# Where the second banks of maxima stand in the attention loop, and how VectorE takes them in the odd slot

## The chip, the core and the metric

The kernel runs on one core of a Trainium2 chip. The metric is the device time of one execution in microseconds. Three runs of the kernel before gave 723.34, 723.61 and 723.65 us; their median is 723.61.

## The reference, cut to what matters

One token mixer with a sliding window, gated by a channel MLP. S = 2048 tokens, D = 512 channels, 32 heads of 16 channels, a window of 256 tokens, 1792 hidden channels.

```
xn = layernorm(x)
q, k, v = split(xn @ wqkv)                       # 32 heads of 16
scores = q @ k^T * 16**-0.5, masked to 0 <= i - j < 256
s = softmax(scores) @ v, heads joined, @ wo
g = silu(gelu(layernorm(xn) @ w1 + b1) @ w2 + b2)
out = x + s * g
```

The change touches one part: the largest score of each query row. The softmax subtracts it, so it must be known before the probabilities of that row are made.

## The kernel before

The attention works on groups of four heads (n = 0 to 7) and blocks of 128 tokens (16 in a group). A query block sees three key blocks: its own, the one before and the one two before; the outer two are masked so that together they make one full block. So 128 units "group, block" run through three stages.

**Maxima** (lines 570 to 592). The scores of one block of queries for four heads go into two tiles of PSUM, of two banks each. The tile `xy` holds three of four parts of each bank pair; `max_first` fills it with matmuls, then VectorE copies the masked half of one block over the other (`copy_predicated`, 128x256) and reduces 768 columns to 6 maxima (`tensor_reduce`). The tile `zo` holds the rest; `max_second` fills columns 0 to 255 of both its banks, and VectorE does the same with a copy of 256 columns and a reduce of 256 columns to 2 maxima. `a` is the index of the bank. The last 256 columns of bank 1 of `zo` are `otb`, the place of the output product. The text calls `xy` the first banks and `zo` the second banks.

**Probabilities** (`prob_part`). TensorE makes transposed scores in the tile `stb`, ScalarE takes the exponential into `pt`, GpSimd zeroes what the mask excludes.

**Output product** (`pv_part`). TensorE multiplies `pt` by the values `vt` into `otb`, and ScalarE copies it to `oraw`, which goes to DRAM.

The loop (line 988) makes one pass u for two blocks, with an even slot t = 2u and an odd slot t = 2u + 1; `pv_part(u)` ends the pass. The maxima run `LEAD` = 12 blocks ahead, so passes 0 to 57 each hold two blocks of maxima. Before the loop, `max_block` does the first 12 blocks. Between these steps the loop spreads fills (`fb`), the projections and other matmuls that TensorE does on the side; `parted` cuts their list into pieces, and `some` issues one. Steps put off by `later` are issued by `run(delayed.pop(...))`; `planned` issues copies and fetches by a table of due times.

The order is written out by hand: the wrapper at line 42 issues each instruction and keeps it in the order of the program on its engine. So line 42 stands in nearly all rows of the profile, and the tiles tell the instructions apart. Semaphores come from the tile library, which sees a tile such as `zo` in its waits.

In the even slot, the order on TensorE was: scores, first banks, a piece of the fills, second banks, more fills. On VectorE: copy of xy, copy of zo, reduce of zo, reduce of xy. In the odd slot TensorE does a piece of fills, second banks, fills, first banks, then the next pass's scores and the output product; VectorE does copy of zo, reduce of zo, copy of xy, reduce of xy.

Of the kernel before, what the change touches and what calls it, by code (L numbers as in the profile page):

```python
# [13 lines left out]
ALU = mybir.AluOpType  # L14
AX = mybir.AxisListType
# [3 lines left out]
P = 128  # L19
# [6 lines left out]
LEAD = 12  # L26
# [23 lines left out]
def mixer_kernel(ctx, tc, x, wqk, wv, wo, w1, b1, w2, b2, out):  # L50


    nc = SimpleNamespace(**{name: Ordered(tc, name) for name in ("tensor", "vector", "scalar", "gpsimd", "sync")})
# [94 lines left out]
    def run(steps):  # L148
        for step in steps:
            step()  # L150
# [31 lines left out]
    zo = psum.tile([P, 2, 512], F32, name="zo")  # L182
# [40 lines left out]
    mask = upper.bitcast(I32).unsqueeze(1).to_broadcast([P, 2, P])  # L223
# [61 lines left out]
    now = [0, 0]  # L285
    delayed = {}
# [263 lines left out]
    def max_place(n, qb):  # L550

        if (n, qb // 4) not in mts:
            mts[n, qb // 4] = small.tile([P, 2, 2, 2, 4], F32, tag="mt", name=f"mt_{n}_{qb}", bufs=2)
        return mts[n, qb // 4].rearrange("q a p i b -> q a (p i) b")[:, :, :, qb % 4]

    def max_scores(out, n, qb, p, parts):

        slot = slots[n % 2]
        for at_, first, count, step in parts:
            for a in (1, 0):  # L560
                r = slice(64 * a, 64 * a + 64)
                row = slot[r, 1, p]
                if first is None:
                    keys = row[:, 0:1].to_broadcast([64, P * count])
                else:
                    keys = row.rearrange("d (b k) -> d b k", k=P)[:, first: first + step * (count - 1) + 1: step]
                nc.tensor.matmul(out[:, a, P * at_: P * (at_ + count)], slot[r, 0, p, P * qb: P * (qb + 1)], keys,
                                 start=True, stop=True)

    def max_second(n, qb):  # L570

        max_scores(zo, n, qb, 1, [(0, qb - 2, 2, 2)] if qb > 1 else [(0, 0, 2, 1)] if qb else [(0, None, 1, 1), (1, 0, 1, 1)])
        own = zo[:, :, P: 2 * P]
        nc.vector.copy_predicated(own, mask, zo[:, :, 0: P])
        nc.vector.tensor_reduce(out=max_place(n, qb)[:, :, 3], in_=own, axis=AX.X, op=ALU.max, negate=True)

    def max_first(n, qb):

        max_scores(xy, n, qb, 0, [(0, qb - 2, 3, 1)] if qb > 1 else [(0, 0, 1, 1), (1, 0, 2, 1)] if qb else
                   [(0, None, 2, 1), (2, 0, 1, 1)])  # L580
        max_scores(xy, n, qb, 1, [(3, qb - 1 if qb else None, 1, 1)])
        nc.vector.copy_predicated(xy[:, :, 2 * P: 3 * P], mask, xy[:, :, 0: P])
        return lambda: nc.vector.tensor_reduce(
            out=max_place(n, qb)[:, :, 0:3], in_=xy[:, :, P: 4 * P].rearrange("q a (i k) -> q a i k", k=P),
            axis=AX.X, op=ALU.max, negate=True)

    def max_block(n, qb):

        rest = max_first(n, qb)
        max_second(n, qb)  # L590
        rest()

    def max_rows(n, c, t):
# [25 lines left out]
    def prob_part(u, part):  # L619

        n, kb = u // 8, 2 * (u % 8)
        if part == 2 and kb == 14:
            return
        slot = slots[n % 2]
        both = stb[0]
        if 16 * n + kb + LEAD >= 16 * NQ and (3 * u + (part + 3) % 3) % 2:
            both = xy
        pt = pp.tile([P, 2, 512], F32, tag="pt", name=f"pt_{u}_{part}")

        def scores(at_, a, p, k, q, w):  # L630
            r = slice(64 * a, 64 * a + 64)
            nc.tensor.matmul(both[:, a, at_: at_ + w], slot[r, 1, p, P * k: P * (k + 1)],
                             slot[r, 0, p, P * q: P * q + w], start=True, stop=True)
        if part < 2:
            w = min(384, S - P * kb)
            for a in (1, 0):
                scores(128, a, part, kb, kb, w)
            for a in (1, 0):
                scores(0, a, part, kb + 1, kb + 1, 128)
            w += 128  # L640
        else:
            w = 512
            for p in range(2):
                for a in (1, 0):
                    scores(256 * p, a, p, kb + 1, kb + 2, 256)
        outs["exp"] = nc.scalar.activation(pt[:, :, 0:w], both[:, :, 0:w], AF.Exp, scale=DH ** -0.5)

        def select(at_, step, pattern, compare, by):
            nc.gpsimd.affine_select(out=at_, in_=at_, pattern=pattern, compare_op=compare, fill=0.0, base=0,
                                    channel_multiplier=by)  # L650
        if part < 2:
            own = pt[:, :, 0:256].rearrange("k a (b q) -> k a b q", b=2)
            select(own, 1, [[0, 2], [0, 2], [1, P]], ALU.is_ge, -1)
            if w == 512:
                select(pt[:, :, 384:512], 1, [[0, 2], [-1, P]], ALU.is_gt, 1)
        else:
            last = pt.rearrange("k a (p q) -> k a p q", p=2)[:, :, :, 128:256]
            select(last, 1, [[0, 2], [0, 2], [-1, P]], ALU.is_gt, 1)
        pts[u, part] = pt
# [154 lines left out]
    n, raw = raws["qk"]  # L814
    nc.gpsimd.tensor_tensor(wqs[0][:, 1], raw, wqs[0][:, 0].bitcast(F32), op=ALU.subtract)
    for j, (raw, cast) in enumerate(zip(raws["v"], (nc.scalar.copy, nc.gpsimd.tensor_copy))):
        cast(wva[:, 0, 2 * j: 2 * j + 2], raw)
        nc.gpsimd.tensor_tensor(wva[:, 1, 2 * j: 2 * j + 2], raw, wva[:, 0, 2 * j: 2 * j + 2].bitcast(F32),
                                op=ALU.subtract)
# [114 lines left out]
    def fill_in(t, half):  # L934
        now[:] = t, half
        run(delayed.pop((t, half), ()))
        for fn, args in fills.get((t, half), ()):
            fn(*args)

    def planned(t):  # L940
        for fn, args in plan.get(t, []):
            fn(*args)

    def ended(t):
        for fn, args in ends.get(t, []):
            fn(*args)

    end = 16 * NQ

    def own_max(part, m):  # L950
        return part(m // 16, m % 16) if m < end else lambda: None

    def own_rows(m, t):
        if 0 <= m < end and m % 4 == 3:
            max_rows(m // 16, m % 16 // 4, t)

    for t in range(-16, 0):
        m = t + LEAD
        if t == -5:
            open_slot(1)  # L960
            for k in range(4):
                at(-4 + k // 2 * 2, clear_part, k)
        fill_in(t, 0)
        planned(t)
        if 4 <= m < LEAD:
            max_block(0, m)
        fill_in(t, 1)
        if t == -1:
            early.close()
            stb.append(attn.enter_context(tc.tile_pool(name="ps_s2", bufs=1, space=PSUM)).tile(  # L970
                [P, 2, 512], F32, name="stb"))
            prob_part(0, 0)
            fill_in(t, 2)
        if 0 <= m < 4:
            max_block(0, m)
        run(lns.get(t, ()))
        own_rows(m, t)
        ended(t)
    def parted(todo, *cuts):

        n = sum(fn.__name__ == "unit" for fn, _ in todo)
        at_ = [0, *(-(-n * k // 20) for k in cuts), len(todo)]
        return [todo[a: b] for a, b in zip(at_, at_[1:])]

    def some(todo):
        for fn, args in todo:
            fn(*args)
    for u in range(end // 2):
        t = 2 * u
        prob_part(u, 1)  # L990
        rest = own_max(max_first, t + LEAD)
        calm[0] = t < end - LEAD
        even, odd = (fills.pop((v, 0), []) for v in (t, t + 1))
        if u % 8:
            parts = parted(even, 5) + parted(odd, 10 if u % 8 == 7 else 5, 20)
        else:
            parts = parted(even + odd, 2, 6, 10, 14)
        now[:] = t, 0
        run(delayed.pop((t, 0), ()))
        some(parts[0])  # L1000
        own_max(max_second, t + LEAD)
        rest()
        planned(t)
        some(parts[1])
        fill_in(t, 1)
        ended(t)
        t += 1
        prob_part(u, 2)
        now[:] = t, 0
        run(delayed.pop((t, 0), ()))  # L1010
        some(parts[2])
        own_max(max_second, t + LEAD)
        some(parts[3])
        planned(t)
        fill_in(t, 1)
        own_max(max_first, t + LEAD)()
        calm[0] = False
        own_rows(t + LEAD, t)
        for fn, args in todo_dve:
            fn(*args)  # L1020
        todo_dve.clear()
        if u % 8:
            some(parts[4])
        if t + 1 < end:
            prob_part(u + 1, 0)
        if u % 8 == 0:
            some(parts[4])
        fill_in(t, 2)
        pv_part(u)
        ended(t)  # L1030
# [29 lines left out]
    for f in range(6, NF, 2):  # L1060
        t = gp.tile([P, 2, 512], F32, tag="ohl", name=f"hr_{f}", bufs=4)
# [452 lines left out]
```

## Time and profile before

| | us |
|---|---|
| median of three runs | 723.61 |
| the profiled execution | 723.22 |
| its span, first to last instruction | 721.1 |
| stretch 60 to 385 (most of the attention loop): TensorE busy | 318.98 of 325.00 |
| the same stretch: VectorE busy | 270.00 |
| the same stretch: ScalarE busy | 237.86 |
| the same stretch: GpSimd busy | 213.55 |

The mean granted TensorE clock of the execution is 0.999 of full speed. PE is TensorE, DVE VectorE, ACT ScalarE, POOL GpSimd. An instruction is named by its output and input tiles; `zo<-qk` are the matmuls of the second banks, `xy<-qk` those of the first, `zo<-pt,vt` the output product. In a timeline the first column is the start and the second the time that the merged group took, both in us. A group of matmuls ends with the tail of its last one, so the next group's start, not the group's end, tells when TensorE handed on. A bracket at a row's end gives the engine's idle time before it and what ended it, as the profile infers it.

### The profile page before, as it was taken

What the parts mean: (1) busy time and instruction counts of PE and PEld (TensorE: products, weight loads), DVE (VectorE), ACT (ScalarE), POOL (GpSimd) and SP (SyncE); (2) the same over time, 40 slices, a digit from 0 to 9 for tenths busy, and PEclk for the clock granted to TensorE, in tenths of its full rate; (3) what the DMA queues carried; (4) which work ended last, traced back from release to release, by engine and by line L of the source; (5) the groups of instructions that cost most, each with busy time, mean ns of one, the idle gap of its engine ahead of it and who ended that gap; (6) DMA issues with size and microseconds to landing.
All of it is one profiled execution on the core that took longest, in us unless ns stands there. A gap on an engine that the chain in (4) does not pass through costs nothing.

```text
span 721.1 us, 17402 instructions
## 1 busy us (share of the span) xinstructions
PE 709.1 (98%) x6704; PEld 565.4 (78%) x6704; DVE 530.6 (74%) x999; ACT 411.3 (57%) x604; POOL 298.9 (41%) x496
## 2 busy tenths in 40 slices
PE   8999999999999999999999999999999999999997
PEld 8998767767678886766767788888888888888886
DVE  7987888988888777888984676347686856767833
ACT  8767777777676676877877735132354644541001
POOL 7344666666566655767777340204203000001102
PEclk9999999999999999999999999999999999999999
DMA  9325455775439976687644549156222312263701
GB/s 305 76 49 128 91 141 151 191 165 131 100 90 265 279 243 212 170 200 196 171 125 146 195 163 288 63 147 218 87 79 97 118 59 87 77 187 116 242 23 58
DMA packets 66273, 106.92 MB, mean 148 GB/s; under 512 B 12624, under 2 KB 21072, under 8 KB 66192
## 3 DMA queue, kind: packets, MB, share of 16 engines
q1 hardware_dynamic: 66192, 105.82, 50.9%
q8 instruction: 53, 0.87, 0.5%
q14 instruction: 28, 0.23, 0.1%
HBM read 54.80 MB, written 33.82 MB: 123 GB/s over the span
## 4 chain that ended last, share of the span: by engine, by line
PE 80%; POOL 8%; DVE 4%; ACT 3%; issue 2%; DMA 2%; SPq 1%; POOLq 0%; ACTq 0%; DVEq 0%
PE acc L42 21%; PE fb L42 13%; PE zo L42 12%; PE p L42 9%; PE s L42 6%; PE h L42 6%; PE stb L42 5%; POOL pt L42 5%; PE xy L42 4%; ACT pt L42 3%; POOL pjr L42 2%; DVE mt L42 2%; PE pv L42 2%; SPq L42 1%; DVE xy L42 1%
## 5 line engine op out<-in xcount | busy, mean ns | idle before, releaser
L42 ACT ACTIVATE pt<-stb 128x1024 f32<-128x1024 f32 (+1 forms) x176 | 177.3, 1007 | 56.5 <-PE stb L42 49.6
L42 POOL TENSOR_SCALAR_AFFINE_SELECT pt<-pt 128x512 f32<-128x512 f32 (+1 forms) x296 | 164.4, 575 | 73.8 <-ACT pt L42 70.9
L42 DVE TENSOR_REDUCE mt<-xy 128x6 f32<-128x768 f32 x128 | 122.0, 953 | 2.0
L42 POOL TENSOR_TENSOR xo<-xo,gated 128x512 f32<-128x512 f32 x15 | 20.0, 1331 | 221.7 <-DVE gated L42 220.7
L42 PE MATMUL fb<-xnT,wqb 64*128 64x512 f32 (+2 forms) x732 | 109.8, 386 | 0.2
L42 PE MATMUL acc<-w,gh 128*128 128x512 f32 x320 | 98.5, 389 | 0.0
L42 PE MATMUL zo<-pt,vt 128*17 128x128 f32 (+1 forms) x1920 | 90.5, 327 | 4.3 <-POOL pjr L42 0.5
L42 PEld LDWEIGHTS zo<-pt,vt 128*17 128x17 f32 x1920 | 52.7, 97 | 37.0 <-issue 4.9
L42 PE MATMUL stb<-qk 64*128 64x384 f32 (+1 forms) x704 | 81.0, 307 | 0.0
L42 DVE COPY_PREDICATED xy<-upper,xy 128x256 f32<-128x256 int32 x128 | 54.1, 423 | 27.5 <-PE xy L42 26.0
L42 PEld LDWEIGHTS stb<-qk 64*128 64x128 f32 x704 | 53.6, 185 | 22.5 <-ACT pt L42 10.3
L42 PEld LDWEIGHTS acc<-w,gh 128*128 128x128 f32 x320 | 60.1, 188 | 12.4
L42 PEld LDWEIGHTS fb<-xnT,wqb 64*128 64x128 f32 (+1 forms) x732 | 61.0, 185 | 6.6 <-PE fb L42 1.0
L42 PE MATMUL xy<-qk 64*128 64x128 f32 (+2 forms) x576 | 62.7, 300 | 0.7 <-DVE mt L42 0.4
L42 PE MATMUL acc<-w,gl 128*128 128x512 f32 x160 | 62.2, 389 | 0.0
L42 DVE TENSOR_REDUCE mt<-zo 128x2 f32<-128x256 f32 x128 | 54.5, 425 | 4.4
L42 DVE COPY_PREDICATED zo<-upper,zo 128x256 f32<-128x256 int32 x128 | 54.2, 423 | 3.8 <-PE zo L42 1.3
L42 PEld LDWEIGHTS xy<-qk 64*128 64x128 f32 x576 | 42.9, 185 | 16.2 <-DVE mt L42 13.7
L42 PE MATMUL p<-xnT 128*128 128x512 f32 x189 | 51.8, 389 | 0.0
L42 PE MATMUL s<-wos,ohl 128*128 128x512 f32 (+1 forms) x204 | 44.3, 376 | 0.0
L42 ACT ACTIVATE gated<-acc 128x512 f32<-128x512 f32 x16 | 8.7, 596 | 61.9 <-DVE acc L42 61.9
L42 DVE TENSOR_TENSOR gl<-g,gh 128x512 fp32r<-128x512 f32 x24 | 17.7, 739 | 34.4 <-ACT gh L42 34.4
(206 smaller groups left out, 1258.0 us busy)
## 6 DMA issues: line engine op xcount, KB each, us to landing
qk<-sh SPq DMA_DIRECT2D x128, 128.0 KB
qk<-pjr SPq DMA_DIRECT2D x64, 128.0 KB
oT_d<-oraw SPq DMA_DIRECT2D x64, 128.0 KB
w_d<-in_w_dram SPq DMA_DIRECT2D x14, 512.0 KB
xt_d<-xnT SPq DMA_DIRECT2D x12, 512.0 KB
x<-in_x_dram SPq DMA_DIRECT2D x16, 256.0 KB
w<-w_d SPq DMA_DIRECT2D x16, 256.0 KB
or<-oT_d SPq DMA_DIRECT2D x16, 256.0 KB
```

What stands on the lines that cost most here:

```text
L42: r = issue(*args, **kwargs)
```

## The change

In the even slot the matmuls of the second banks, with VectorE's copy and reduce, stand directly behind the first banks, ahead of the first piece of fills; the delayed steps of that slot are issued ahead of both. In the odd slot VectorE takes the second banks one by one: `max_second` gets a list of slices of the banks, makes one copy for each and then one reduce for each, with bank 1, where the output lies, first. The even slot and `max_block` still pass one slice of both banks.

```diff
-    def max_second(n, qb):
+    def max_second(n, qb, halves):
 
         max_scores(zo, n, qb, 1, [(0, qb - 2, 2, 2)] if qb > 1 else [(0, 0, 2, 1)] if qb else [(0, None, 1, 1), (1, 0, 1, 1)])
-        own = zo[:, :, P: 2 * P]
-        nc.vector.copy_predicated(own, mask, zo[:, :, 0: P])
-        nc.vector.tensor_reduce(out=max_place(n, qb)[:, :, 3], in_=own, axis=AX.X, op=ALU.max, negate=True)
+        for a in halves:
+            nc.vector.copy_predicated(zo[:, a, P: 2 * P], mask[:, a], zo[:, a, 0: P])
+        for a in halves:
+            nc.vector.tensor_reduce(out=max_place(n, qb)[:, a, 3], in_=zo[:, a, P: 2 * P], axis=AX.X, op=ALU.max, negate=True)
...
         prob_part(u, 1)
+        now[:] = t, 0
+        run(delayed.pop((t, 0), ()))
         rest = own_max(max_first, t + LEAD)
+        own_max(lambda n, qb: max_second(n, qb, (slice(0, 2),)), t + LEAD)
+        if rest:
+            rest()
...
-        now[:] = t, 0
-        run(delayed.pop((t, 0), ()))
         some(parts[0])
-        own_max(max_second, t + LEAD)
-        rest()
         planned(t)
...
         some(parts[2])
-        own_max(max_second, t + LEAD)
+        own_max(lambda n, qb: max_second(n, qb, (slice(1, 2), slice(0, 1))), t + LEAD)
         some(parts[3])
```

On TensorE, in the even slot of a pass (xy first banks, zo second banks, fb_111 and fb_112 the two banks of the fills):

```order
 L42 MATMUL xy<-qk_94 128x384 x2
 L42 MATMUL xy<-qk_94 128x128 x2
+L42 MATMUL zo<-qk_94 128x256 x2
 L42 MATMUL fb_112<-xnT,wqb_789 128x512
 L42 MATMUL fb_111<-xnT,wqb_789 128x512
-L42 MATMUL zo<-qk_94 128x256 x2
 L42 MATMUL fb_112<-xnT,wqb_789 128x512
 L42 MATMUL fb_111<-xnT,wqb_789 128x512
```

The matmuls of the second banks moved past one pair of fills; nothing else moved there.

On VectorE, the even slot and the odd slot of one pass before, with the semaphores that each row waits for (mt holds the maxima; DVE_49 is VectorE's own semaphore):

```order
L42 COPY_PREDICATED xy<-upper,xy 128x2x128 [waits DVE_49,PE_49]
L42 COPY_PREDICATED zo<-upper,zo 128x2x128 [waits PE_49,Activation_49]
L42 TENSOR_REDUCE mt_4_2987<-zo 128x2 [waits DVE_49]
L42 TENSOR_REDUCE mt_4_2987<-xy 128x2x3
L42 COPY_PREDICATED zo<-upper,zo 128x2x128 [waits DVE_49,PE_49]
L42 TENSOR_REDUCE mt_4_2987<-zo 128x2 [waits DVE_49]
L42 COPY_PREDICATED xy<-upper,xy 128x2x128 [waits PE_49]
L42 TENSOR_REDUCE mt_4_2987<-xy 128x2x3 [waits DVE_49]
```

And the same stretch now:

```order
L42 COPY_PREDICATED xy<-upper,xy 128x2x128 [waits DVE_49,PE_49]
L42 COPY_PREDICATED zo<-upper,zo 128x2x128 [waits PE_49,Activation_49]
L42 TENSOR_REDUCE mt_12_2650<-zo 128x2 [waits DVE_49]
L42 TENSOR_REDUCE mt_12_2650<-xy 128x2x3
L42 COPY_PREDICATED zo<-upper,zo 128x128 [waits DVE_49,PE_49]
L42 COPY_PREDICATED zo<-upper,zo 128x128 [waits DVE_49]
L42 TENSOR_REDUCE mt_12_2650<-zo 128x1 [waits DVE_49]
L42 TENSOR_REDUCE mt_12_2650<-zo 128x1
L42 COPY_PREDICATED xy<-upper,xy 128x2x128 [waits PE_49]
L42 TENSOR_REDUCE mt_12_2650<-xy 128x2x3 [waits DVE_49]
```

VectorE's order in the even slot is as before; in the odd slot two rows became four. Counted out in the built program, the second copy waits for the first copy and the first reduce for the second copy. The output product at the end of the pass waits for a count that VectorE reaches with the last of the four.

More of the change, by code (lines that the diff above doesn't have):

```diff
@@ L589, in max_block @@
         rest = max_first(n, qb)
-        max_second(n, qb)
+        max_second(n, qb, (slice(0, 2),))
         rest()
@@ L950, in own_max @@
     def own_max(part, m):
-        return part(m // 16, m % 16) if m < end else lambda: None
+        return part(m // 16, m % 16) if m < end else None
     def own_rows(m, t):
@@ L1015, in mixer_kernel @@
         fill_in(t, 1)
-        own_max(max_first, t + LEAD)()
+        rest = own_max(max_first, t + LEAD)
+        if rest:
+            rest()
         calm[0] = False
```

## The prediction

> **What bounds the kernel now.** The page comes first, and it points to TensorE:
>
> ```profile
> PE 709.1 (98%) x6704; PEld 565.4 (78%) x6704; DVE 530.6 (74%) x999; ACT 411.3 (57%) x604; POOL 298.9 (41%) x496
> PE 80%; POOL 8%; DVE 4%; ACT 3%; issue 2%; DMA 2%; SPq 1%; POOLq 0%; ACTq 0%; DVEq 0%
> ```
>
> TensorE is busy for 98% of the span, and the chain that ended last lies on it for 80%. Neither number says that the attention loop runs at TensorE's pace, because a matmul's busy time includes its tail and hides a wait of some tenths. So I read one pass of the loop engine by engine. The change touches VectorE, so the timeline of VectorE is next, in pass 27 (start us, duration us, engine, instruction):
>
> ```profile
> 208.99 0.43 DVE L42 COPY_PREDICATED xy<-upper,xy 128x256 f32<-128x256 int32 x1 [1.07 <-PE xy L42]
> 209.46 0.43 DVE L42 COPY_PREDICATED zo<-upper,zo 128x256 f32<-128x256 int32 x1
> 209.93 0.42 DVE L42 TENSOR_REDUCE mt<-zo 128x2 f32<-128x256 f32 x1
> 210.27 0.95 DVE L42 TENSOR_REDUCE mt<-xy 128x6 f32<-128x768 f32 x1
> 211.13 0.42 DVE L42 COPY_PREDICATED zo<-upper,zo 128x256 f32<-128x256 int32 x1
> 211.58 0.42 DVE L42 TENSOR_REDUCE mt<-zo 128x2 f32<-128x256 f32 x1
> 211.93 0.42 DVE L42 COPY_PREDICATED xy<-upper,xy 128x256 f32<-128x256 int32 x1
> 212.38 0.96 DVE L42 TENSOR_REDUCE mt<-xy 128x6 f32<-128x768 f32 x1
> ```
>
> The first four rows are the even slot, the last four the odd one. VectorE waits 1.07 us for the even slot's first banks (xy) and then never stops. The same stretch on TensorE:
>
> ```profile
> 206.73 1.49 PE L42 MATMUL zo<-pt,vt 128*17 128x256 f32 x32
> 208.16 0.51 PE L42 MATMUL stb<-qk 64*128 64x384 f32 x4
> 208.50 0.46 PE L42 MATMUL xy<-qk 64*128 64x384 f32 x4
> 208.78 0.46 PE L42 MATMUL fb<-xnT,wqb 64*128 64x512 f32 x2
> 209.07 0.28 PE L42 MATMUL zo<-qk 64*128 64x256 f32 x2
> ...
> 210.41 0.38 PE L42 MATMUL zo<-qk 64*128 64x256 f32 x2
> ...
> 211.32 0.46 PE L42 MATMUL xy<-qk 64*128 64x384 f32 x4
> 211.61 0.46 PE L42 MATMUL stb<-qk 64*128 64x384 f32 x4
> 212.16 0.70 PE L42 MATMUL zo<-pt,vt 128*17 128x256 f32 x9
> ```
>
> The row at 206.73 is one pass's output product (probabilities times V, into a corner of zo), the row at 212.16 the next one's. It starts 0.16 us behind the end of VectorE's odd reduce of zo (211.58 + 0.42 = 212.00). That is a wait: the scores ahead of it took 0.55 us to hand on (211.61 to 212.16). The same two rows, first and last in the loop:
>
> ```profile
> 70.73 0.42 DVE L42 TENSOR_REDUCE mt<-zo 128x2 f32<-128x256 f32 x1
> 71.30 0.63 PE L42 MATMUL zo<-pt,vt 128*17 128x256 f32 x8
> ...
> 378.33 0.42 DVE L42 TENSOR_REDUCE mt<-zo 128x2 f32<-128x256 f32 x1
> 378.90 0.63 PE L42 MATMUL zo<-pt,vt 128*17 128x256 f32 x8
> ```
>
> The distance is 0.15 us in both, and in 45 of the 57 output products of passes 1 to 57. Against them stands one of the other 12:
>
> ```profile
> 251.07 0.42 DVE L42 TENSOR_REDUCE mt<-zo 128x2 f32<-128x256 f32 x1
> 251.78 0.45 PE L42 MATMUL stb<-qk 64*128 64x384 f32 x4
> 252.16 0.41 PE L42 MATMUL zo<-pt,vt 128*17 128x256 f32 x4
> ```
>
> Here the reduce was done 0.67 us earlier and the scores handed on after 0.38 us. So a waiting pass loses 0.55 - 0.38 = 0.17 us of TensorE, and **the 45 passes go round a ring**: output product, scores and xy matmuls on TensorE (206.73 to 208.99, 2.26 us), six VectorE instructions (208.99 to 212.00, 3.01 us), the handover (0.16 us); 5.43 us in all. TensorE's fills have room inside it. What VectorE's stretch gains or loses is the time, 45 times.
>
> **The even slot.** The copy of zo starts at 209.46, when the copy of xy has been over for 0.04 us. What starts it is TensorE: zo's matmuls begin at 209.07, 0.39 us earlier. A pass with longer fills shows the same 0.39 us (230.85 to 231.24) with a wider gap:
>
> ```profile
> 230.64 0.43 DVE L42 COPY_PREDICATED xy<-upper,xy 128x256 f32<-128x256 int32 x1 [1.02 <-PE xy L42]
> 230.85 0.28 PE L42 MATMUL zo<-qk 64*128 64x256 f32 x2
> 231.24 0.43 DVE L42 COPY_PREDICATED zo<-upper,zo 128x256 f32<-128x256 int32 x1 [0.17 <-ACT pt L42]
> ```
>
> The profile names ScalarE for that gap; ScalarE's copy of the output, the other thing waited for, was long done. Moved directly behind xy, zo's matmuls start at about 208.78 instead of 209.07, and release the copy at 208.78 + 0.39 = 209.17, before the copy of xy ends at 209.42. What the copy does then is seen in pass 8, where VectorE came late and zo was ready:
>
> ```profile
> 106.42 0.40 DVE L42 COPY_PREDICATED xy<-upper,xy 128x256 f32<-128x256 int32 x1
> 106.73 0.42 DVE L42 COPY_PREDICATED zo<-upper,zo 128x256 f32<-128x256 int32 x1
> 107.18 0.42 DVE L42 TENSOR_REDUCE mt<-zo 128x2 f32<-128x256 f32 x1
> ```
>
> It starts 0.09 us before its forerunner ends (106.42 + 0.40 = 106.82), so it overlaps. From the start of the copy of xy to the reduce of zo it took 209.93 - 208.99 = 0.94 us; it will take 0.43 - 0.09 + 0.42 + 0.03 = 0.79 us. **The even slot gains 0.15 us.** On TensorE the moved matmuls now wait for ScalarE's copy of the output with the fills queued behind them:
>
> ```profile
> 208.33 0.37 ACT L42 COPY oraw<-zo 128x256 f32<-128x256 f32 x1 [0.57 <-PE zo L42]
> ```
>
> It ends at 208.70, before they are reached at 208.78, so the wait is some hundredths at most; the 0.17 us of room hides them, and without that cover they would be paid in each pass. The order of ScalarE, GpSimd and the DMA queue does not change, the delayed steps included.
>
> [...]
>
> **The odd slot.** One copy and one reduce become two copies and two reduces of half the width, and the program sets a wait at each step but the last: the second copy waits for the first, the first reduce for the second copy, and only the second reduce follows without a wait. The output product waits for a VectorE count that is reached with the **last** reduce, that of the other bank; taking the output's bank first releases nothing. No row has a half-width copy or reduce, so I price it from its neighbours (busy, then mean ns):
>
> ```profile
> L42 DVE TENSOR_REDUCE mt<-xy 128x6 f32<-128x768 f32 x128 | 122.0, 953 | 2.0
> L42 DVE TENSOR_REDUCE mt<-zo 128x2 f32<-128x256 f32 x128 | 54.5, 425 | 4.4
> L42 DVE COPY_PREDICATED zo<-upper,zo 128x256 f32<-128x256 int32 x128 | 54.2, 423 | 3.8 <-PE zo L42 1.3 <-ACT pt L42 0.2
> L42 DVE STREAM_TRANSPOSE mT<-mh 128x32 f32<-128x32 f32 x32 | 6.8, 212 | 16.9 <-POOL mh L42 16.2 <-DMA qk<-sh 0.6
> L42 DVE TENSOR_SCALAR ve<-mvs 128x1 f32<-128x1 f32 x9 | 1.4, 154 | 0.5
> ```
>
> From 256 to 768 columns a reduce grows by 528 ns, 1.03 ns a column, so 128 columns fewer save 132 ns: 425 becomes 293 and 423 becomes 291. From below, the one-column row gives 154 + 127 x 1.03 = 285 ns, the 32-column transpose 212 + 96 x 1.03 = 311 ns. I take 0.29 us; the ends are 0.285 and 0.311. A wait between two of them costs 0.03 us (211.13 + 0.42 to 211.58), and no wait gives 0.08 us back (the reduce of xy at 210.27 starts before 209.93 + 0.42 = 210.35). Before: 0.42 + 0.03 + 0.42 = 0.87 us. After: four times 0.29, two waits and one overlap, 1.16 + 0.06 - 0.08 = 1.14 us. **The odd slot costs 0.27 us**, all of it ahead of the output product. Behind it stand the odd copy and reduce of xy; they keep their distance to the output product and delay nobody else.
>
> [...]
>
> **The sum.** A waiting pass goes from 5.43 to 5.43 - 0.15 + 0.27 = 5.55 us. Of the 45, 35 have the gap of 0.04 us: 35 x 0.12 = 4.2 us. Five (passes 2, 10, 18, 26, 50), whose second banks take two pairs of matmuls, have a gap of 0.10 us and gain more: 5 x 0.065 = 0.3 us. In three (12, 42, 52) the copy of zo overlaps already and gains nothing: 3 x 0.27 = 0.8 us. Pass 25, gap 0.17 us, comes out even, and pass 49, where zo stands behind a fill that waits for a bank, gains some 0.2 us. The other 12 have 0.09 us of room or more and stay. Together 4.2 + 0.3 + 0.8 - 0.2 = 5.1 us. The profiled execution took 723.22 us (span 721.1 and 2.1 around it), so **728.3 us**; the median of the runs shown is 723.61, 0.4 above it.
>
> **Rivals.**
> - *The copy of zo does not overlap.* Then the even slot gains its gap alone, 0.04 us, and a pass loses 0.23 us: 45 x 0.23 = 10.4 us, 733.6 us. Pass 8 speaks against it, and five more passes like it. 8%.
> - *Not slower: half-width instructions cost less than the line through the rows says.* Four of them stand in the ring, so a pass breaks even where each takes 0.26 us instead of 0.29, and gains below that. At 0.26 us the time stays at about 723 us. For it: no row shows the shape. Against it: 154 ns at one column and 425 at 256 lie on one line with 953 at 768. 9%.
> - *Faster: the waits go by bank*, the second copy starts without waiting and the output product is let go by the first reduce. The ring would shrink by more than TensorE's room, so by 0.17 us a pass: 45 x 0.17 = 7.7 us, 715.6 us. Against it stand the waits in the order above. 4%.
>
> **How the numbers follow.** My forecast has 79%. Its own range: four half-width instructions at 0.285 to 0.311 us give 4 x (-0.005 to +0.02) a pass, -0.9 to +3.6 us over 45; with the even gain uncertain by 0.04 us a pass, 1.8 us, it is 725.5 to 732. The range given, 723.5 to 734, takes in the first rival and part of the second and leaves out the third. A measurement of this kernel tells about 0.2% (1.4 us) from no change. Slower by more than that: the forecast but for its low edge, and the first rival, 82%. Within: most of the second rival and that edge, 11%. Faster: the third rival and the rest of the second, 7%.
>
> **What would show it.** In the profile after: half-width copies and reduces at 0.29 us; the copy of zo in the even slot starting 0.09 us before the copy of xy ends; the output product still 0.15 us behind the last reduce; passes of 5.55 us, with the scores ahead of the output product handing on after 0.67 us instead of 0.55. Wrong would be: an output product that starts behind the first reduce, a copy of zo that still waits for TensorE, or passes that another engine ends.

## The result, and the profile after

The changed kernel took 728.22 us (median of four runs, 728.09 to 728.45), against 723.48 us for the kernel before (median of four runs, 723.26 to 723.65). The ratio is 1.0066 with a 95% interval of 1.0049 to 1.0084: slower by 0.7%. The profiled execution took 728.23 us, its span is 726.2 us, and the mean granted clock is 1.000.

From the page after, the busy times and the shares of the chain that ended last:

```profile
PE 705.4 (97%) x6704; PEld 567.9 (78%) x6704; DVE 539.7 (74%) x1115; ACT 411.6 (57%) x604; POOL 299.3 (41%) x496
PE 74%; DVE 15%; issue 6%; ACT 1%; POOL 1%; DMA 1%; SPq 0%; ACTq 0%; DVEq 0%
```

TensorE is busy 3.7 us less in a span that is 5.1 us longer, and VectorE's share of the chain has gone from 4% to 15%. More of the waiting shows now as idle time of TensorE: 13.8 us ahead of the output product's matmuls, where the page before has 4.3. The waits of TensorE have a row that stood nowhere before (total, times, longest, in us):

```profile
PE zo L42 <- DVE mt L42: 12.4, 38, 0.4
```

This is the output product, written into `zo`, waiting for VectorE's maxima `mt`. Its place in a pass is read from the timeline of VectorE after, in pass 27, the pass that the prediction shows:

```profile
211.53 0.43 DVE L42 COPY_PREDICATED xy<-upper,xy 128x256 f32<-128x256 int32 x1 [1.07 <-PE xy L42]
211.87 0.42 DVE L42 COPY_PREDICATED zo<-upper,zo 128x256 f32<-128x256 int32 x1
212.32 0.42 DVE L42 TENSOR_REDUCE mt<-zo 128x2 f32<-128x256 f32 x1
212.66 0.95 DVE L42 TENSOR_REDUCE mt<-xy 128x6 f32<-128x768 f32 x1
213.53 0.61 DVE L42 COPY_PREDICATED zo<-upper,zo 128x128 f32<-128x128 int32 x2
214.18 0.49 DVE L42 TENSOR_REDUCE mt<-zo 128x1 f32<-128x128 f32 x2
```

and from TensorE's timeline after, in the same pass:

```profile
209.28 1.50 PE L42 MATMUL zo<-pt,vt 128*17 128x256 f32 x32 [0.18 <-DVE mt L42]
...
211.03 0.45 PE L42 MATMUL xy<-qk 64*128 64x384 f32 x4
211.32 0.36 PE L42 MATMUL zo<-qk 64*128 64x256 f32 x2
211.52 1.09 PE L42 MATMUL fb<-xnT,wqb 64*128 64x512 f32 x8
...
212.95 0.28 PE L42 MATMUL zo<-qk 64*128 64x256 f32 x2
213.07 0.86 PE L42 MATMUL fb<-xnT,wqb 64*128 64x512 f32 x6
213.77 0.41 PE L42 MATMUL xy<-qk 64*128 64x384 f32 x4
214.01 0.51 PE L42 MATMUL stb<-qk 64*128 64x384 f32 x4
214.81 0.41 PE L42 MATMUL zo<-pt,vt 128*17 128x256 f32 x4 [0.30 <-DVE mt L42]
```

Three things are to be seen. In the even slot the copy of zo starts at 211.87, 0.09 us before the copy of xy ends (211.53 + 0.43 = 211.96), and from the start of the copy of xy to the reduce of zo it is 0.79 us, where it was 0.94. In the odd slot the four half-width instructions run from 213.53 to 214.67, 1.14 us where two took 0.87. And the output product at 214.81 stands 0.14 us behind the last of them. The pass took 214.81 - 209.28 = 5.53 us, where it took 5.43.

The chain that ended last, in the same pass (start, duration, what), now runs through the odd slot's VectorE work, which it passed by before:

```profile
213.53 0.30 DVE zo L42
213.82 0.02 issue
213.85 0.31 DVE zo L42
214.15 0.02 issue
214.18 0.50 DVE mt L42 x2
214.68 0.14 issue
214.81 1.24 PE zo L42 x21
```

The two copies stand one behind the other with the 0.02 to 0.03 us of a wait between them; the two reduces overlap, 0.50 us for both. The groups of VectorE over the whole kernel after, with the new shapes (busy us, mean ns):

```profile
L42 DVE COPY_PREDICATED zo<-upper,zo 128x128 f32<-128x128 int32 x116 | 33.7, 290 | 3.3 <-PE zo L42 1.3
L42 DVE TENSOR_REDUCE mt<-zo 128x2 f32<-128x256 f32 x70 | 29.8, 426 | 2.4
L42 DVE COPY_PREDICATED zo<-upper,zo 128x256 f32<-128x256 int32 x70 | 29.5, 421 | 0.0
L42 DVE TENSOR_REDUCE mt<-zo 128x1 f32<-128x128 f32 x116 | 28.3, 286 | 2.0
```

Half the columns cost 290 and 286 ns, against 421 and 426 for all of them.

### The profile page after: what moved, and what is told of

It is laid out like the page before. It is cut to its first block, busy times and chain, and to the rows that moved or that the text cites. A ratio compares the mean times of both kernels' runs of the same rounds, so it can differ in the third digit from the quotient of the medians.

```text
span 726.2 us, 17518 instructions
## 1 busy us (share of the span) xinstructions
PE 705.4 (97%) x6704; PEld 567.9 (78%) x6704; DVE 539.7 (74%) x1115; ACT 411.6 (57%) x604; POOL 299.3 (41%) x496
## 4 chain that ended last, share of the span: by engine, by line
PE 74%; DVE 15%; issue 6%; ACT 1%; POOL 1%; DMA 1%; SPq 0%; ACTq 0%; DVEq 0%
PE acc L42 21%; PE zo L42 12%; PE fb L42 9%; PE p L42 9%; DVE mt L42 7%; PE s L42 6%; PE h L42 6%; DVE zo L42 6%; PE stb L42 4%; PE xy L42 4%; DVE xy L42 2%; PE pv L42 2%; POOL pt L42 1%; DMA x<-in_x_dram 1%; POOL mh L42 1%
## 5 line engine op out<-in xcount | busy, mean ns | idle before, releaser
L42 PE MATMUL zo<-pt,vt 128*17 128x128 f32 (+1 forms) x1920 | 90.5, 327 | 13.8 <-DVE mt L42 12.4
L42 PE MATMUL fb<-xnT,wqb 64*128 64x512 f32 (+2 forms) x732 | 101.4, 380 | 0.1
L42 DVE COPY_PREDICATED zo<-upper,zo 128x256 f32<-128x256 int32 x186 | 63.2, 340 | 3.3 <-PE zo L42 1.3
L42 PE MATMUL xy<-qk 64*128 64x128 f32 (+2 forms) x576 | 61.2, 294 | 0.4 <-DVE mt L42 0.4
L42 DVE TENSOR_REDUCE mt<-zo 128x2 f32<-128x256 f32 x186 | 58.1, 338 | 4.4
L42 ACT COPY oraw<-zo 128x256 f32<-128x256 f32 x64 | 23.9, 374 | 39.2 <-PE zo L42 31.4
```

The costliest lines, as they stand in the source:

```text
L42: r = issue(*args, **kwargs)
```

## The experiments

Each kernel differs from the changed one by the edit shown, and each is compared with runs of the kernel before made on the same chip: median 723.31 us for the two parts alone, the output's bank last and the two tiles; 723.59 us for the two halves of the split and the two tiles with the output's bank last. "The loop" below is the time from the start of the output product of pass 0 to that of pass 57, read from each profile: 312.37 us before (66.53 to 378.90), 317.48 us after (66.62 to 384.10). So the loop holds +5.11 us of what the change costs. The starts are rounded, so sums of such figures can be off by 0.01 or 0.02.

### One part at a time

The even slot's move alone; the odd slot takes both banks at once again:

```diff
-        own_max(lambda n, qb: max_second(n, qb, (slice(1, 2), slice(0, 1))), t + LEAD)
+        own_max(lambda n, qb: max_second(n, qb, (slice(0, 2),)), t + LEAD)
```

> The even slot as in the change, the odd slot as before (one copy and one reduce of both banks). Theory of the ring (VectorE's stretch sets the pass): each of the 45 waiting passes loses 0.15 us of VectorE's stretch, which still fits into TensorE's room of 0.17 us, so 45 x 0.15 = 6.8 us less than before, about 717 us, and the output product still 0.15 us behind the reduce of zo in most passes. Rival (the order of the fills on TensorE gains nothing, the even slot was never waited for): 723.5 us as before.

It took 717.19 us, 6.12 us less than the kernel before, ratio 0.9916 (0.9902 to 0.9929). VectorE's odd copy and reduce of zo in pass 27 of this kernel:

```profile
207.85 0.42 DVE L42 COPY_PREDICATED zo<-upper,zo 128x256 f32<-128x256 int32 x1
208.31 0.42 DVE L42 TENSOR_REDUCE mt<-zo 128x2 f32<-128x256 f32 x1
```

and TensorE's output products around them:

```profile
203.59 1.50 PE L42 MATMUL zo<-pt,vt 128*17 128x256 f32 x32
...
208.34 0.50 PE L42 MATMUL stb<-qk 64*128 64x384 f32 x4
208.88 0.63 PE L42 MATMUL zo<-pt,vt 128*17 128x256 f32 x8
```

The output product still stands 0.15 us behind the reduce (208.73), so the ring is only shorter: 5.29 us here, 5.28 in the middle one of the 57 passes. The move gains 0.15 us a pass, as priced, and the loop is 6.53 us shorter.

The other part alone; the even slot stands in the order of before, the odd slot as in the change:

```diff
         prob_part(u, 1)
-        now[:] = t, 0
-        run(delayed.pop((t, 0), ()))
         rest = own_max(max_first, t + LEAD)
-        own_max(lambda n, qb: max_second(n, qb, (slice(0, 2),)), t + LEAD)
-        if rest:
-            rest()
...
+        now[:] = t, 0
+        run(delayed.pop((t, 0), ()))
         some(parts[0])
+        own_max(lambda n, qb: max_second(n, qb, (slice(0, 2),)), t + LEAD)
+        if rest:
+            rest()
```

> The odd slot as in the change (two copies and two reduces of half the width), the even slot as before. Theory of the ring: 45 passes longer by 0.27 us, 12.2 us, about 735.6 us. Rival (the even slot has no part in it, the odd slot alone makes the change's 4.7 us): 728.2 us.

It took 735.49 us, 12.18 us more than before, ratio 1.0167 (1.0153 to 1.0181). VectorE in pass 27 of this kernel, from the even slot's copies to the odd slot's reduces:

```profile
215.22 0.43 DVE L42 COPY_PREDICATED xy<-upper,xy 128x256 f32<-128x256 int32 x1 [1.07 <-PE xy L42]
215.69 0.43 DVE L42 COPY_PREDICATED zo<-upper,zo 128x256 f32<-128x256 int32 x1
...
217.36 0.61 DVE L42 COPY_PREDICATED zo<-upper,zo 128x128 f32<-128x128 int32 x2
218.01 0.49 DVE L42 TENSOR_REDUCE mt<-zo 128x1 f32<-128x128 f32 x2
```

The gap of 0.04 us ahead of the copy of zo is back (215.22 + 0.43 = 215.65), and the odd slot takes 1.14 us. The loop is 12.26 us longer, the middle pass 5.68 us instead of 5.43. So the two parts work in opposite directions, and the change is nearly their sum: -6.53 + 12.26 = +5.73 us against +5.11. Pass by pass the two add up within 0.07 us but for passes 25 and 49, where together they overstate by 0.40 us.

### The output's bank last

The change takes the output's bank first. Here it comes last, with nothing else altered:

```diff
-        own_max(lambda n, qb: max_second(n, qb, (slice(1, 2), slice(0, 1))), t + LEAD)
+        own_max(lambda n, qb: max_second(n, qb, (slice(0, 1), slice(1, 2))), t + LEAD)
```

> The change with the banks of the odd slot taken in the other order, the output's bank last. Theory (the output product waits for the last of the four instructions, whichever bank it is of): 728.2 us as after. Rival (the output's bank first lets the output product start before the other reduce has ended): later by one reduce less its overlap, 0.2 us a pass, 45 x 0.2 = 9 us, about 737 us.

It took 728.74 us, ratio 1.0073 (1.0059 to 1.0086), and the loop is 5.09 us longer than before, against 5.11 in the changed kernel. The order of the banks does nothing, as it should if the output product waits for the last reduce whichever bank that reads.

### Which half of the split costs what

In one kernel only the copies are split, in the other only the reduces; the even slot keeps its move in both.

```diff
         for a in halves:
             nc.vector.copy_predicated(zo[:, a, P: 2 * P], mask[:, a], zo[:, a, 0: P])
-        for a in halves:
+        for a in (slice(0, 2),):
             nc.vector.tensor_reduce(out=max_place(n, qb)[:, a, 3], in_=zo[:, a, P: 2 * P], axis=AX.X, op=ALU.max, negate=True)
```

> The change, but in the odd slot only the copies are of half the width, each waiting for the one before; one reduce of both banks follows. Theory (a half-width instruction with a wait behind it costs 0.29 + 0.03 us, one without a wait only what it does not overlap, 0.2 us): the copies take 0.29 + 0.04 + 0.30 instead of 0.42 us, 0.20 us more a pass than the even slot alone (717.2 us), the reduce is as before; 0.06 us less a pass than after, about 725.4 us. Rival (each of the two added instructions costs the same, wait or not): halfway between the even slot alone and after, 722.7 us.

```diff
-        for a in halves:
+        for a in (slice(0, 2),):
             nc.vector.copy_predicated(zo[:, a, P: 2 * P], mask[:, a], zo[:, a, 0: P])
```

> The change, but in the odd slot only the reduces are of half the width, the second without a wait; one copy of both banks goes ahead. Theory: the reduces take 0.29 + 0.28 - 0.08 = 0.49 us instead of 0.42, 0.06 us more a pass than the even slot alone, about 720.0 us. Rival (each of the two added instructions costs the same, wait or not): 722.7 us.

With the copies split it took 725.43 us, ratio 1.0026 (1.0017 to 1.0036); with the reduces split 719.56 us, ratio 0.9945 (0.9929 to 0.9962). The odd slot's copies and reduce where only the copies are split, on VectorE:

```profile
211.74 0.61 DVE L42 COPY_PREDICATED zo<-upper,zo 128x128 f32<-128x128 int32 x2
212.39 0.42 DVE L42 TENSOR_REDUCE mt<-zo 128x2 f32<-128x256 f32 x1
```

and where only the reduces are:

```profile
208.74 0.42 DVE L42 COPY_PREDICATED zo<-upper,zo 128x256 f32<-128x256 int32 x1
209.19 0.49 DVE L42 TENSOR_REDUCE mt<-zo 128x1 f32<-128x128 f32 x2
```

Two half-width copies take 0.61 us where one whole takes 0.42; two half-width reduces take 0.49. Both split one instruction into two of nearly the same length (290 and 286 ns). The difference is that the second copy waits for the first and the second reduce doesn't. Against the even slot's move alone (-6.12 us against its own before) the copies cost 1.84 + 6.12 = 7.96 us, 0.18 us in each of 45 passes, and the reduces 6.12 - 4.03 = 2.09 us, 0.05 us in each. The loops say 8.67 and 2.63 us (314.52 and 308.48 us, against 305.85 with the move alone), 0.19 and 0.06 us a pass. That is nearly all of the 11.62 us that both halves together cost there.

### Two tiles instead of one

If the price is the waits, which the tile library keeps for `zo` as a whole, then the same split should cost little where each bank is a tile of its own. Here `zo` is two tiles of one bank, and all second banks, in both slots and in `max_block`, are taken one by one, the output's first; every other use of `zo` names one of the two tiles:

```diff
-    zo = psum.tile([P, 2, 512], F32, name="zo")
-    otb = zo[:, 1, 256:512]
+    zo = [psum.tile([P, 512], F32, name=f"zo{a}") for a in range(2)]
+    otb = zo[1][:, 256:512]
...
-        for a in halves:
-            nc.vector.copy_predicated(zo[:, a, P: 2 * P], mask[:, a], zo[:, a, 0: P])
-        for a in halves:
-            nc.vector.tensor_reduce(out=max_place(n, qb)[:, a, 3], in_=zo[:, a, P: 2 * P], axis=AX.X, op=ALU.max, negate=True)
+        for a in (1, 0):
+            nc.vector.copy_predicated(zo[a][:, P: 2 * P], mask[:, a], zo[a][:, 0: P])
+        for a in (1, 0):
+            nc.vector.tensor_reduce(out=max_place(n, qb)[:, a, 3: 4], in_=zo[a][:, P: 2 * P], axis=AX.X, op=ALU.max, negate=True)
```

In the built program the second copy then waits for its own matmul alone, each reduce for its own copy, and the output product for the reduce of its own bank.

> The change with zo as two tiles of one bank each, so that the waits go by bank; both slots (and the blocks ahead of the loop) take the banks one by one, the output's first. The program now lets the second copy follow without a wait and the output product wait for the first reduce alone. Theory (waits, not the count of instructions, make the odd slot dear): the four instructions of the even slot take 4 x 0.2 = 0.8 us to the reduce of xy, as the two did; the odd slot lets the output product go after 0.39 + 0.29 = 0.68 us instead of 1.14. VectorE's stretch falls below TensorE's, which then sets the pass: 45 x 0.17 = 7.7 us less than before, about 716 us, and the output product no longer 0.15 us behind a reduce. Rival (each added VectorE instruction costs its time in the ring, with or without a wait): 0.27 us more a pass than after, about 740 us.

It took 712.74 us, ratio 0.9852 (0.9838 to 0.9865): 1.5% faster than the kernel before and 2.1% faster than the changed one (712.74 / 728.22 = 0.979). It is the fastest of all that were run, and 3 us faster than the theory said. VectorE in pass 27 of this kernel:

```profile
203.62 0.43 DVE L42 COPY_PREDICATED xy<-upper,xy 128x256 f32<-128x256 int32 x1 [1.00 <-PE xy L42]
203.95 0.49 DVE L42 COPY_PREDICATED zo<-upper,zo 128x128 f32<-128x128 int32 x2
...
205.61 0.48 DVE L42 COPY_PREDICATED zo<-upper,zo 128x128 f32<-128x128 int32 x2
206.00 0.48 DVE L42 TENSOR_REDUCE mt<-zo 128x1 f32<-128x128 f32 x2
```

and TensorE in the same pass:

```profile
201.36 1.50 PE L42 MATMUL zo<-pt,vt 128*17 128x256 f32 x32
...
205.03 0.29 PE L42 MATMUL zo<-qk 64*128 64x256 f32 x2
205.15 0.87 PE L42 MATMUL fb<-xnT,wqb 64*128 64x512 f32 x6
...
206.10 0.49 PE L42 MATMUL stb<-qk 64*128 64x384 f32 x4
206.52 0.73 PE L42 MATMUL zo<-pt,vt 128*17 128x256 f32 x12
```

The four half-width instructions of the odd slot now run from 205.61 to 206.48, 0.87 us, no more than the two whole ones before. The output product at 206.52 is only 0.04 us behind the last of them, and the scores ahead of it handed on after 0.42 us, near the 0.38 of a pass that doesn't wait. The ring is open, and the page of this kernel shows TensorE as the bound (shares of the chain that ended last):

```profile
PE 96%; DVE 2%; DMA 1%; ACT 1%; SPq 0%; issue 0%; POOL 0%; ACTq 0%
```

The same two tiles with the output's bank last tell the waits per bank from the missing waits between neighbours:

```diff
-        for a in (1, 0):
+        for a in (0, 1):
             nc.vector.copy_predicated(zo[a][:, P: 2 * P], mask[:, a], zo[a][:, 0: P])
-        for a in (1, 0):
+        for a in (0, 1):
             nc.vector.tensor_reduce(out=max_place(n, qb)[:, a, 3: 4], in_=zo[a][:, P: 2 * P], axis=AX.X, op=ALU.max, negate=True)
```

> zo as two tiles, both slots one bank at a time, but the output's bank last. Theory (with waits by bank the output product waits for the reduce of its own bank, now the second): VectorE's stretch to the output product is 0.2 us longer than with the output's bank first; TensorE's passes there had 0.03 to 0.09 us to spare, so 0.11 to 0.17 us a pass, 45 x 0.13 = 6 us, about 718.5 us. Rival (the order of the banks makes no difference here either): 712.7 us.

It took 716.58 us, ratio 0.9902 (0.9888 to 0.9917). The odd reduces of zo in this kernel, on VectorE:

```profile
207.52 0.48 DVE L42 TENSOR_REDUCE mt<-zo 128x1 f32<-128x128 f32 x2
```

and the output product on TensorE:

```profile
208.15 0.81 PE L42 MATMUL zo<-pt,vt 128*17 128x256 f32 x13
```

The output product waits again, 0.15 us behind the second reduce (208.00). With two tiles the bank order matters: 4.4 us in the loop (305.92 against 301.48), 3.6 us in the medians with each set against its own runs of the kernel before. With one tile it made no difference. The effect is smaller than the theory said; the loop is as long as with the move alone (305.92 us, there 305.85), so splitting without waits between the halves cost nothing here, and letting the output product go by the first reduce brought the rest.

## Why the prediction was right, point by point

The forecast was 728.3 us, measured 728.22. The longer time was forecast as 5.1 us; it is 5.01 between the two profiled executions and 4.74 between the medians. The mechanism and its terms held. Some sizes beside them were off; two of them don't enter the sum, and the errors of the third cancelled.

- **The ring of 45 passes.** Shown. Whatever VectorE's stretch gained or lost came out as time with both signs, -6.53 and +12.26 us, and the output product kept its distance of 0.14 to 0.15 us from the reduce in each kernel where it waits for the last one. That TensorE was busy for 98% before did not keep the move alone from gaining 0.8%.
- **The even slot, 0.15 us gained.** Shown: 0.94 to 0.79 us in pass 27, and 5.43 to 5.28 us in the middle pass of the kernel with the move alone. The copy overlaps its forerunner by 0.09 us, as in pass 8 before, so the first rival fell.
- **The odd slot, 0.27 us lost.** Shown: 0.87 to 1.14 us in pass 27. The price of 0.29 us for an instruction that no row had came out at 290 and 286 ns, so the second rival, which needed 0.26, fell.
- **The output product waits for the last of the four.** Shown: the bank order does nothing with one tile. The third rival, waits by bank, fell as a reading of this change; with two tiles it is what happens.
- **The sum.** The 45 waiting passes gave +5.14 us, 5.1 were forecast; the other 12 gave -0.04, the stretch ahead of the loop +0.10. That last figure is scatter, since the same stretch gave -0.22 to +0.70 us in the five experiments with one tile, whose code there is the same. So the agreement to 0.1 us in the whole time is partly luck; that of the 45 passes is not. Passes 12, 42 and 52 gave 0.25 to 0.26 each (0.27 said), pass 25 gave +0.02 (even, said), pass 49 gave -0.28 (-0.2 said).
- **Off: the other 12 passes each by itself.** They were to stay. Pass 31 lost 0.23 us: its output product waits now, 0.15 us behind the reduce. Its room was 0.09 us, less than the 0.12 that a pass loses by the two terms, and the even slot's gain does not count in it: both before and after, VectorE stands idle ahead of the odd copy of zo (0.09 us, and 0.43 now), which starts 0.32 to 0.33 us behind TensorE's odd matmuls of zo. The kernels with one part alone show it: +0.16 us in this pass with the odd slot's change, +0.06 and no gain with the even slot's move. Passes 16, 24, 32 and 40 gave 0.08 to 0.13 us each back, and nearly as much with the move alone. That the 12 add up to near nothing is luck.
- **Off: the moved matmuls' wait for ScalarE.** Some hundredths at most were said. They hand on after 0.20 us now (211.32 to 211.52), where they took 0.12 before (209.07 to 209.19), 0.08 us more. In the built program the one thing that they wait for is ScalarE's copy of the output, which ends at 211.24, 0.08 us ahead of them; that the 0.08 us more is this wait is the author's estimate from these times. TensorE's room hides it, as was said: the move alone still gains 0.15 us in the middle pass.
- **Off: TensorE's room in a pass, 0.17 us.** It was larger by 0.13 us. Here is the odd slot of pass 27 on TensorE before, of which the prediction left the second row out:

```profile
210.41 0.38 PE L42 MATMUL zo<-qk 64*128 64x256 f32 x2
210.63 0.86 PE L42 MATMUL fb<-xnT,wqb 64*128 64x512 f32 x6
```

and in the kernel with the odd slot's change alone, where the even slot is as late as before:

```profile
216.65 0.37 PE L42 MATMUL zo<-qk 64*128 64x256 f32 x2
216.86 0.85 PE L42 MATMUL fb<-xnT,wqb 64*128 64x512 f32 x6
```

The matmuls of zo took 0.22 and 0.21 us to hand on. They take 0.12 in the changed kernel (212.95 to 213.07), with the two tiles (205.03 to 205.15) and with the even slot's move alone (207.28 to 207.40). They may write `zo` only when the even slot's reduce of it has ended: before, that was at 209.93 + 0.42 = 210.35, just ahead of them. The odd matmuls of xy, which wait for the even reduce of xy, show the same on a smaller scale: 0.29 us before (211.32 to 211.61), 0.24 now (213.77 to 214.01). So further waits lay under the first. Once the even slot runs early, they go, and what they gave up is added to the wait at the output product. The scores there hand on after 0.80 us (214.01 to 214.81), not after the 0.67 of the forecast, and with the move alone after 0.54 (208.34 to 208.88), as before. The price of the third rival, 715.6 us, was too high: 45 x 0.30 = 13.5 us would give 710, and the two tiles, where the scores still take 0.42 us, brought 10.9 in the loop. That these waits end with the even slot's reduces is read from the times and from what the built program waits for: the two kernels with the late even slot show them, the seven with the early one don't. The sum didn't use the room, so the forecast didn't suffer.

- **A small sum.** The forecast's own range takes both of its uncertainties at the low end and only one at the high end; with both, the high end would be 733.7 us, still inside the range given.

## What to carry to other kernels

TensorE, busy for 98% of the span before, still waited in 45 of 57 passes (the scores handed on after 0.55 us in pass 27, after 0.38 in a pass that didn't wait). A constant distance between one engine's end and another's start, in pass after pass, showed the ring (0.15 us here), and work inside the ring changed the time, by -6.53 and +12.26 us in the loop. Splitting an instruction in two cost more than the whole (2 x 290 against 421 ns; 0.48 or 0.49 us for two copies that overlap), and still more where a wait stood between the halves (0.61 us); it paid only where someone could go on after the first half, and so only where the waits were kept for the halves (the loop took 301.48 us there, 305.92 with the output's bank last, 305.85 without the split). Look at what the built program waits for before taking an order in the source for an order of release.

## What the runs showed of the hardware

Two neighbours among VectorE's copies and reduces of xy and zo overlap by 0.08 to 0.09 us where no wait holds the second (211.87 against 211.96 in pass 27 after), and stand 0.03 us apart where it waits for the first (0.02 in the view of the chain): some 0.12 us for each wait, though the instructions are only 0.29 us long. So four half-width instructions took 1.14 us with the waits of one tile and 0.87 us with those of two, as much as the two whole ones. Two half-width copies take 0.61 us with the wait and 0.48 or 0.49 without.
